# A piece of one V block sent as eight four-row transfers in a two-layer decode kernel

## The chip, the cores and the metric

The kernel runs on one core of a Trainium2 chip. The metric is the time of one execution on the device in microseconds (us), lower is better; a kernel is run several times and the median counts.

## The reference

One token passes through two layers. Each layer is attention over a cache, then a small dense block, both with a layer norm before and a residual after. Both layers use the same caches and weights.

```python
def _A_ref(x, k_cache, v_cache, wq, wo):        # 32 heads of 128, 4096 keys, x is 1 x 512
    q = (x @ wq).reshape(B, Sq, H, Dh).transpose(0, 2, 1, 3)
    scores = jnp.einsum("bhqd,bhkd->bhqk", q, k_cache) * (Dh ** -0.5)
    p = softmax(scores, axis=-1)
    o = jnp.einsum("bhqk,bhkd->bhqd", p, v_cache)
    return o.transpose(0, 2, 1, 3).reshape(B, Sq, H * Dh) @ wo
...
x = x + _A_ref(_layernorm(x), A_k_cache, A_v_cache, A_wq, A_wo)
x = x + _B_ref(_layernorm(x), B_w1, B_b1, B_w2, B_b2)    # gelu(x @ w1 + b1) @ w2 + b2, 1376 wide
x = x + _A_ref(...)
x = x + _B_ref(...)
```

## The kernel before

The 32 heads are worked on in 8 groups (`G`) of 4 heads (`J`). For a group the host lays K out as 128 rows of 64 KB (a row is one of a head's 128 dimensions) and V as 128 rows of 64 KB: row p holds keys p, p + 128, p + 256 and so on of the four heads. A block of 64 KB a row is eight chunks (`C`) of 2048 floats (`NC`); a chunk holds four pieces of 512 floats (`U`), and a piece is one run of 128 keys, 4 heads by 128 dimensions. One group reads K (8 MB), V (8 MB) and a row block of weights (2 MB: the group's wo and the next group's wq). Everything is float32.

All data goes into one large SBUF tile, `arena`. Its first three blocks are homes for K and V in turn (`k_home`, `v_home`); behind them lie spare chunks, `HELD` (first the start weights, at the layer's end the dense block's w1) and `PAIR` (wo and wq). `load` (L85) issues a transfer on SP's queue and keeps it in program order, so SP issues K, V and w of a group, then K, V and w of the next, each as soon as its home is free. The issue of w waits for the previous group's wo to be used up, which L311 does.

In the first six groups of layer 0 (the variable `pairs` is set) the V block isn't multiplied on TensorE. The softmax gives the weights `pt` with a key to a partition. ScalarE scales chunks 4 to 7 in 64 small instructions (`weighted_by_act`, L269), VectorE scales chunks 0 to 3 in four large ones (`weighted`, L274), and VectorE adds the chunks up: `add_pair` (L279) adds two chunks to two others and is called three times, 4096 columns each, and one addition of 2048 columns (L574) leaves the sum in the group's first chunk. Between these additions stands the next group's query (`queries`, L215 to L223). The sum over the partitions is taken late, in the middle of the next group's scores: `sum_over_keys` (L283, TensorE), `scaled_out` (L287 to L292) and `summed_wo` (L309 and L311, VectorE), and after that SP may issue the next w. The other groups multiply V on TensorE (L262).

GpSimd (POOL) prepares an identity matrix and a few constants at the start. Layer 1 goes through the groups in the opposite order and reads K and V again; it keeps what of the last group is still on the chip.

Of the kernel before, what the change touches and what calls it, by code (L numbers as in the profile page):

```python
# [13 lines left out]
AF = mybir.ActivationFunctionType  # L14
ALU = mybir.AluOpType
AX = mybir.AxisListType

P = 128
# [4 lines left out]
J = 4  # L23
C = 8
# [3 lines left out]
U = 512  # L28
KEPT = 6

NC = 4 * U
BLOCK = 8 * NC
# [3 lines left out]
HELD = SPARE + 2 * NC  # L36
PAIR = HELD + 4 * FJ * J
ARENA = PAIR + 2 * NC
SMALLS = 324
AHEAD = 64  # L40
X_AT, B1_AT, B2_AT = 0, 8, 8 + FB
K2_HOME = 12 * NC

# [11 lines left out]
WHOLE, HALVES = ((0, 8),), ((0, 4), (4, 8))  # L55
# [2 lines left out]


@with_exitstack  # L60
def decode_layers(ctx: ExitStack, tc: tile.TileContext, k, v, w, w1, w2, out):
    nc = tc.nc
    const = ctx.enter_context(tc.tile_pool(name="const", bufs=1))
    work = ctx.enter_context(tc.tile_pool(name="work", bufs=1))
# [2 lines left out]
    def ctile(name, *shape):  # L67
        return const.tile([P, *shape], F32, name=name)
# [14 lines left out]
    arena = const.tile([P, ARENA], F32, name="arena")  # L83

    def load(at, src):  # L85
        t = arena[:, at : at + src.shape[-1]]
        tc.keep_in_program_order(nc.sync.dma_start(t, src))  # L87
        return t

    def pin(ins):  # L90
        tc.keep_in_program_order(ins)

    def chunk(t, i=0):
        return t[:, NC * i : NC * (i + 1)].rearrange("p (j n) -> p j n", j=4)
# [12 lines left out]
    def free_now(layer, n):  # L107

        if layer == 0:
            at = HELD + 2 * NC  # L110
        elif n == 0:
            at = 6 * NC
            return arena[:, at : at + U], arena[:, 11 * NC : 11 * NC + 4 * 129]
        else:
            at = 9 * NC if n == 1 else 14 * NC
        return arena[:, at : at + U], arena[:, at + U : at + U + 4 * 129]
# [14 lines left out]
    ahead = load(HELD, w[row][:, : AHEAD + NC])  # L131
    wq_first = chunk(ahead[:, AHEAD:])

    ident = ctile("ident", P)
    make_identity(nc, ident)
    nc.vector.memset(negmean, -1.0 / D)
# [8 lines left out]
    pK = [psum.tile([P, U], F32, name=f"pK{j}") for j in range(KEPT - 1)]  # L145
# [7 lines left out]
    mx, mb = small("mx", 32), small("mb", 32)  # L153
    for t in (zq, mx, mb):
        nc.vector.memset(t, 0.0)

    def of_32(t, n, i=0):
        return t[:, : 32 * n].rearrange("p (c q) -> p c q", q=32)[:, :, i]
# [76 lines left out]
    def softmax(sc, nsc, p, hold):  # L235
        top = nc.vector.tensor_reduce(mx[:, 0:1], pS, axis=AX.X, op=ALU.max)  # L236
        if hold:
            pin(top)
        mt, m, bias = small("mt", 32), small("m"), small("lr", 32)
        nc.vector.transpose(mt, mx)  # L240
        nc.vector.tensor_reduce(m, mt[:, :C], axis=AX.X, op=ALU.max)
        nc.vector.tensor_scalar(mb[:, :C], m.to_broadcast([P, C]), nsc, None, op0=ALU.mult)
        nc.vector.transpose(bias, mb)  # L243
        nc.scalar.activation(p, pS, AF.Exp, bias=bias[:, 0:1], scale=sc, accum_out=mx[:, 0:1])  # L244
        for b in range(4):
            nc.tensor.transpose(pT[:, b].rearrange("p j r -> p (j r)"), p[:, P * b : P * (b + 1)], ident)  # L246
        pt = work.tile([P, J, C, 4], F32, name="pt")
        nc.vector.tensor_copy(pt, pT[:, :, :, :C].rearrange("p b j c -> p j c b"))
        lt, l, lr, rl = small("mt", 32), small("l"), small("lr", 32), small("rl")
        nc.vector.transpose(lt, mx)  # L250
        nc.vector.tensor_reduce(l, lt[:, :C], axis=AX.X, op=ALU.add)
        nc.vector.tensor_copy(lt, l.to_broadcast([P, 32]))
        nc.vector.transpose(lr, lt)
        nc.vector.reciprocal(rl, lr[:, 0:1])
        return pt, rl
# [4 lines left out]
    def values(i, pt, vt, c, of=C):  # L260
        for j in range(J):
            nc.tensor.matmul(pO[32 * j : 32 * j + 4, :], pt[:, j, c, :], by_head(vt)[:, j],  # L262
                             start=(i == 0), stop=(i == of - 1))

    def weighted_by_act(pt, t, c):
        for b in range(4):
            for j in range(J):
                own = by_head(t)[:, j, b]
                nc.scalar.activation(own, own, AF.Copy, scale=pt[:, j, c, b : b + 1])  # L269
# [3 lines left out]
        weight = pt[:, :, c, :].rearrange("p j b -> p b j")[:, :, :, None].to_broadcast([P, 4, J, DH])  # L273
        nc.vector.tensor_tensor(own, own, weight, op=ALU.mult)  # L274

    def add_pair(at, to, by):

        a, b = (arena[:, at + NC * c : at + NC * (c + 2)] for c in (to, by))
        pin(nc.vector.tensor_tensor(a, a, b, op=ALU.add))  # L279

    def sum_over_keys(t):
# [142 lines left out]
    here = {}  # L424

    def stream(what, g, pieces, base):

        for a, b in pieces:
            t = load(base + NC * a, part(k if what == "k" else v, g, a, b))
            for c in range(a, b):  # L430
                here[what, g, c] = chunk(t, c - a)
                yield c, here[what, g, c]
# [7 lines left out]
    for layer in range(2):  # L440
# [17 lines left out]
        r = rstd_of(ss, pN[:, 1:2], True)  # L458
# [5 lines left out]
        for n, g in enumerate(order):  # L464
            first, final = n == 0, n == G - 1
            pairs = None
            if layer == 0 and n < G - 2:
                pairs = PAIRS[0]
            if layer == 1 and 1 < n < G - 2:
                pairs = PAIRS[1][n % 2]  # L470

            k_home, v_home = ((2 * n + i) % 3 * BLOCK for i in (1, 2))
            if layer == 1:
                k_home, v_home = K2_HOME if n == 2 else 15 * NC, 6 * NC * (n % 2)
# [28 lines left out]
            p, ot = free_now(layer, n)  # L503
            if layer == 1 and first:
                z = queries(n + 1, xc_l, wq_next, pO)
                nc.scalar.copy(v_next(STAY + U * KEPT - U), pB)
            pt, rl = softmax(sc, nsc, p, held)
            if final:
                nc.scalar.activation(small("m"), rl, AF.Gelu_apprx_tanh)

            if layer == 1 and n == 0:
                for c in range(C):
                    values(c, pt, here["v", g, c], c)
            elif layer == 1 and n == 1:
                for c in range(C):
                    values(c, pt, here["v", g, c], c)

                for pieces, base in ((((0, 4),), K2_HOME), (((4, 6),), SPARE - 4 * NC)):
                    for _ in stream("k", order[2], pieces, base):
                        pass  # L520
            elif final:
                last_v = chunk(arena[:, v_home + BLOCK - NC : v_home + BLOCK])
                for _ in range(FILL - 1 if layer == 1 else 0):
                    idle(t, pS)
                for c, t in stream("v", g, LAST, v_home):
                    values(c, pt, t, c, C - 1)
                    if c == C - 2:
                        others = scaled_out(rl, ot)
                    for _ in range(LAST_IDLE.get(c, 0) * (1 + layer)):
                        idle(t, pS, 512 >> layer)  # L530
                for a, b in END_PARTS[layer]:
                    at = BLOCK - NC + U * a
                    load(v_home + at, v[g][:, at : BLOCK - NC + U * b])
                for c in range(C):
                    here["v", g, c] = chunk(arena[:, v_home + NC * c : v_home + NC * (c + 1)])
            else:
                for c, t in stream("v", g, WHOLE, v_home):
                    for i in range(KEPT - 1):
                        if layer == 0 and n == G - 2 and c == (STAY + U * i) // NC:
                            nc.scalar.copy(pK[i], t[:, STAY // U % J + i - J * (c - STAY // NC), :])  # L540
                    if pairs is None:
                        values(c, pt, t, c)
            if pairs:
                first_pair = pairs[0]
                for c in pairs[2:]:
                    for i in (0, 1):
                        weighted_by_act(pt, here["v", g, c + i], c + i)
                for c in pairs[:2]:
                    for i in (0, 1):
                        weighted(pt, here["v", g, c + i], c + i)  # L550
                add_pair(v_home, *pairs[:2])
# [3 lines left out]
            elif final:  # L555
                at = PAIR + NC * layer
# [9 lines left out]
            else:  # L566
                t = load(PAIR, of_w(wo_at(g) if layer == 0 else wq_at(g - 1), 2))
                wo_t, wq_next = (chunk(t, i) for i in ((0, 1) if layer == 0 else (1, 0)))
            if pairs:
                total, other = here["v", g, first_pair], here["v", g, first_pair + 1]  # L570
                z = queries(n + 1, xc_l, wq_next, pS, short=True,
                            between=lambda: add_pair(v_home, first_pair, pairs[2]))
                add_pair(v_home, first_pair, pairs[3])
                pin(nc.vector.tensor_tensor(total, total, other, op=ALU.add))  # L574

                def late_sum(rl=rl, ot=ot, wt=wo_t, total=total):
                    sum_over_keys(total)
                    summed_wo(scaled_out(rl, ot), wt, ot[:, :U])

                def late_out(ot=ot, n=n):  # L580
                    add_out(ot[:, :U], n)

                late = late_sum, late_out
                continue
# [24 lines left out]
        at = work.tile([P, P], F32, name="pt")  # L609
# [78 lines left out]
```

## Time and profile before

| what | value |
|---|---|
| median of 3 runs | 674.22 us (674.05 to 674.25) |
| profiled execution | 673.33 us |
| its span, first to last instruction | 671.6 us |
| busy in the span: TensorE, VectorE, ScalarE, GpSimd | 299.7, 407.1, 215.4, 5.2 us |
| moved by DMA | 285.29 MB, mean 425 GB/s |

Busy time is that of instructions on an engine within the profiled execution's span. The profiled execution takes some 2 us more than its span, for what lies before the first and after the last instruction.

### The profile page before, as it was taken

How to read it: one execution, taken by the hardware profiler on the slowest of the kernel's cores; microseconds unless marked ns; L12 is line 12 of the kernel's file. 1: busy time of each engine (PE TensorE's matmuls, PEld its weight loads, DVE VectorE, ACT ScalarE, POOL GpSimd, SP SyncE). 2: the span in 40 equal slices, each digit the busy share in tenths (PEclk: the TensorE clock that was granted, in tenths of full speed). 3: DMA queues.
4: the chain of work that ended last, by engine and by line, in shares of the span. 5: the costliest groups of instructions: out<-in, count | busy, mean ns of one | idle time of the engine just before them, and what ended most of it. 6: DMA issues, size and time to landing. Idle time of an engine off the chain costs nothing.

```text
span 671.6 us, 6013 instructions
## 1 busy us (share of the span) xinstructions
PE 299.7 (45%) x2236; PEld 79.7 (12%) x2236; DVE 407.1 (61%) x510; ACT 215.4 (32%) x697; POOL 5.2 (1%) x26
## 2 busy tenths in 40 slices
PE   1511703415116053165768986704316025065597
PEld 1000100101001010011114311101001001011124
DVE  3059679498696886971322313288597694973513
ACT  0047074190560823802011200083290650910010
POOL 1000000000000000000000000000000000000000
PEclk9965755757558557578689998655757559557799
DMA  9999999999999999999999999999999999999997
GB/s 377 437 437 438 435 437 437 403 461 437 437 437 397 444 426 434 433 429 426 425 415 399 422 422 438 437 433 433 431 433 437 437 430 402 462 426 414 431 414 286
DMA packets 11556, 285.29 MB, mean 425 GB/s; under 512 B 1284, under 2 KB 1288, under 8 KB 3720
## 3 DMA queue, kind: packets, MB, share of 16 engines
q1 hardware_dynamic: 11528, 284.92, 99.1%
q8 instruction: 17, 0.28, 0.2%
q14 instruction: 11, 0.09, 0.0%
HBM read 284.92 MB, written 0.00 MB: 424 GB/s over the span
## 4 chain that ended last, share of the span: by engine, by line
DMA 64%; PE 17%; DVE 15%; issue 1%; another core or an unknown queue 1%; SPq 1%; ACT 0%; DVEq 0%; ACTq 0%
DMA arena<-in_v 37%; DMA arena<-in_k 24%; PE pS L232 8%; DVE arena L274 7%; PE pO L262 5%; DMA arena<-in_w 4%; DVE arena L279 3%; DVE arena L311 2%; PE pO L283 1%; DVE arena L287 1%; DVE arena L215 1%; SPq L87 1%; PE pB L323 1%; DVE arena L309 0%
## 5 line engine op out<-in xcount | busy, mean ns | idle before, releaser
L269 ACT ACTIVATE arena<-arena,pt 128x128 f32<-128x128 f32 x640 | 188.0, 387 | 50.8 <-DMA arena<-in_v 48.1
L232 PE MATMUL pS<-arena,smalls 128*8 128x512 f32 x1024 | 147.0, 727 | 78.4 <-DMA arena<-in_k 74.3
L279 DVE TENSOR_TENSOR arena<-arena 128x4096 f32<-128x4096 f32 x30 | 132.6, 4420 | 0.3
L274 DVE TENSOR_TENSOR arena<-arena,pt 128x2048 f32<-128x2048 f32 x40 | 89.0, 2287 | 36.8 <-DMA arena<-in_v 35.7
L217 PE MATMUL pS<-arena,smalls 128*128 128x512 f32 x20 | 20.7, 1140 | 202.5 <-DVE arena L215 202.5
L244 ACT ACTIVATE arena<-pS,smalls 128x512 f32<-128x512 f32 x16 | 12.4, 777 | 289.4 <-DVE smalls L243 289.4
L287 DVE STREAM_TRANSPOSE arena<-pO 128x512 f32<-128x512 f32 x16 | 11.5, 717 | 97.4 <-PE pO L262 61.9
L262 PE MATMUL pO<-arena,pt 128*4 128x512 f32 x368 | 48.9, 666 | 11.8 <-DMA arena<-in_v 11.0
L232 PEld LDWEIGHTS pS<-arena,smalls 128*8 128x8 f32 x1024 | 29.8, 102 | 198.6 <-issue 177.3
L236 DVE TENSOR_REDUCE smalls<-pS 128x1 f32<-128x512 f32 x16 | 11.0, 687 | 64.1 <-PE pS L232 64.1
L215 DVE SCALAR_TENSOR_TENSOR arena<-arena,smalls 128x512 f32<-128x512 f32 x45 | 33.8, 752 | 1.6
L311 DVE SCALAR_TENSOR_TENSOR arena<-arena,smalls 128x512 f32<-128x512 f32 x39 | 29.3, 752 | 1.4
L217 PEld LDWEIGHTS pS<-arena,smalls 128*128 128x128 f32 x20 | 5.0, 311 | 206.2 <-DVE arena L215 206.2
L315 PE MATMUL pB<-arena,smalls 128*1 128x512 f32 x26 | 14.7, 648 | 29.0 <-DVE arena L311 29.0
L246 PE MATMUL pO<-ident,arena 128*128 128x128 f32 x64 | 13.4, 344 | 28.1 <-ACT arena L244 27.8
L574 DVE TENSOR_TENSOR arena<-arena 128x2048 f32<-128x2048 f32 x10 | 22.9, 2292 | 0.3
L382 ACT ACTIVATE smalls<-smalls 128x4 f32<-128x4 f32 (+1 forms) x6 | 1.2, 205 | 44.0 <-DVE smalls L375 25.6
L262 PEld LDWEIGHTS pO<-arena,pt 128*4 128x4 f32 x368 | 9.8, 93 | 44.8 <-issue 42.4
L250 DVE STREAM_TRANSPOSE smalls<-smalls 128x32 f32<-128x32 f32 x16 | 3.4, 212 | 17.5 <-ACT arena L244 17.5
L246 PEld LDWEIGHTS pO<-ident,arena 128*128 128x128 f32 x64 | 8.4, 167 | 42.1 <-ACT arena L244 36.7
L244 ACT ACT_TABLE_LOAD x1 | 1.3, 1283 | 36.9 <-DVE smalls L243 36.9
L438 PE MATMUL pS<-arena,ident 128*8 128x256 f32 (+1 forms) x34 | 11.9, 454 | 0.5 <-DVE pt L367 0.5
(115 smaller groups left out, 183.6 us busy)
## 6 DMA issues: line engine op xcount, KB each, us to landing
arena<-in_w SPq DMA_DIRECT2D x13, 2048.0 KB, 12.5
arena<-in_k SPq DMA_DIRECT2D x6, 4096.0 KB, 21.3
arena<-in_v SPq DMA_DIRECT2D x2, 4096.0 KB, 25.1
arena<-in_w SPq DMA_DIRECT2D x6, 1024.0 KB, 30.9
arena<-in_v SPq DMA_DIRECT2D x2, 2048.0 KB, 37.0
arena<-in_k SPq DMA_DIRECT2D x2, 2048.0 KB, 13.4
arena<-in_w SPq DMA_DIRECT2D x7, 512.0 KB, 9.3
arena<-in_v SPq DMA_DIRECT2D x3, 1024.0 KB, 46.3
```

The costliest lines, as they stand in the source:

```text
L215: pin(nc.vector.scalar_tensor_tensor(t, wt[:, c, :], xc[:, c : c + 1], t, op0=ALU.mult, op1=ALU.add))
L217: pin(nc.tensor.matmul(at, one.to_broadcast([P, P]), t, start=True, stop=True))
L232: pin(nc.tensor.matmul(pS[32 * j : 32 * j + C, :], z[:, j, C - 1 - c : 2 * C - 1 - c], kt[:, j, :], start=(c == 0), stop=(c == C - 1)))
L246: nc.tensor.transpose(pT[:, b].rearrange("p j r -> p (j r)"), p[:, P * b : P * (b + 1)], ident)
L262: nc.tensor.matmul(pO[32 * j : 32 * j + 4, :], pt[:, j, c, :], by_head(vt)[:, j], start=(i == 0), stop=(i == of - 1))
L269: nc.scalar.activation(own, own, AF.Copy, scale=pt[:, j, c, b : b + 1])
L274: nc.vector.tensor_tensor(own, own, weight, op=ALU.mult)
L279: pin(nc.vector.tensor_tensor(a, a, b, op=ALU.add))
L287: nc.vector.transpose(ot[:, :512], pO)
L311: pin(nc.vector.scalar_tensor_tensor(t, wt[:, d, :], on[:, d : d + 1], t, op0=ALU.mult, op1=ALU.add))
L315: pin(nc.tensor.matmul(pB[0:1, :], one, t, start=n == 0, stop=n == G - 2))
L574: pin(nc.vector.tensor_tensor(total, total, other, op=ALU.add))
```

## The change

The last piece (128 keys of each of the four heads, 512 floats a row) of the V block of group 4, the fifth, no longer comes with the block in layer 0. The host lays the same 256 KB out a second time, as an array `m` of 48 rows of 8 KB, in which rows 0 to 15 and 32 to 47 hold data: a row there holds the four heads' values of four keys. Eight transfers bring them into `low`, an area of 48 partitions by 2048 columns that POOL clears at the start. Each takes 4 rows, four partitions apart: rows 0, 4, 8, 12; then 1, 5, 9, 13; and so on, and the same from row 32. Two of them are issued on SP's queue behind V in each of the groups 0 to 3. In group 4 the V block is loaded without its last 512 columns; the weights of the moved keys are turned onto the 48 partitions by four TensorE transposes and a copy (`low_weights`), ScalarE scales `low` in 16 small instructions and leaves out the 4 of the piece that is gone (`weighted_low`), the third `add_pair` is 512 columns shorter, and VectorE adds `low` to the first 48 partitions of the group's sum. A few scratch places move. Layer 1 reads the V block as before.

```diff
+LOW = 48
+MOVED_OF = 4
+MOVED_AT = HELD + NC + AHEAD
+MOVED_ROWS = [slice(32 * h + q, 32 * h + q + 13, 4) for h in range(2) for q in range(4)]
...
         if layer == 0:
-            at = HELD + 2 * NC
+            at = MOVED_AT + NC
...
+    low = arena[:LOW, MOVED_AT : MOVED_AT + NC]
+    nc.gpsimd.memset(low, 0.0)
     ident = ctile("ident", P)
     make_identity(nc, ident)
...
+    low_pt = arena[:, PAIR - 4 * J : PAIR]
...
-    def weighted_by_act(pt, t, c):
-        for b in range(4):
+    def low_weights(p):
+        at = pK[0][:LOW]
+        for i in range(4):
+            first = 3 * P + 64 * (i // 2) + 16 * (i % 2)
+            nc.tensor.transpose(at[:, P * i : P * (i + 1)], p[:, first : first + LOW], ident)
+        t = low_pt[:LOW].rearrange("p (i j) -> p i j", i=4)
+        nc.vector.tensor_copy(t, at.rearrange("p (i j r) -> p i j r", i=4, j=J)[:, :, :, C - 1])
+        return t
+
+    def weighted_low(t):
+        own = low.rearrange("p (i j d) -> p i j d", i=4, j=J)
+        for i in range(4):
+            for j in range(J):
+                nc.scalar.activation(own[:, i, j], own[:, i, j], AF.Copy, scale=t[:, i, j : j + 1])
+
+    def weighted_by_act(pt, t, c, of=4):
+        for b in range(of):
...
-    def add_pair(at, to, by):
-
-        a, b = (arena[:, at + NC * c : at + NC * (c + 2)] for c in (to, by))
+    def add_pair(at, to, by, short=0):
+
+        a, b = (arena[:, at + NC * c : at + NC * (c + 2) - short] for c in (to, by))
         pin(nc.vector.tensor_tensor(a, a, b, op=ALU.add))
...
             pt, rl = softmax(sc, nsc, p, held)
+            dealt = layer == 0 and n == MOVED_OF
+            if dealt:
+                pt_low = low_weights(p)
...
-                for c, t in stream("v", g, WHOLE, v_home):
+                if dealt:
+                    load(v_home, v[g][:, : BLOCK - U])
+                    pieces = [(c, chunk(arena[:, v_home + NC * c : v_home + NC * (c + 1)])) for c in range(C)]
+                    here.update({("v", g, c): t for c, t in pieces})
+                else:
+                    pieces = stream("v", g, WHOLE, v_home)
+                for c, t in pieces:
...
+            if layer == 0 and n < MOVED_OF:
+                for rows in MOVED_ROWS[2 * n : 2 * n + 2]:
+                    pin(nc.sync.dma_start(low[rows], m[rows]))
             if pairs:
                 first_pair = pairs[0]
                 for c in pairs[2:]:
                     for i in (0, 1):
-                        weighted_by_act(pt, here["v", g, c + i], c + i)
+                        weighted_by_act(pt, here["v", g, c + i], c + i, 3 if dealt and c + i == C - 1 else 4)
+                if dealt:
+                    weighted_low(pt_low)
...
-                add_pair(v_home, first_pair, pairs[3])
+                add_pair(v_home, first_pair, pairs[3], U if dealt else 0)
                 pin(nc.vector.tensor_tensor(total, total, other, op=ALU.add))
+                if dealt:
+                    of_low = arena[:LOW, v_home + NC * first_pair : v_home + NC * (first_pair + 1)]
+                    pin(nc.vector.tensor_tensor(of_low, of_low, low, op=ALU.add))
...
+    moved = arrays["v"][MOVED_OF, :, BLOCK - U : BLOCK].reshape(2, 2, 2, 16, U)
+    arrays["m"] = np.zeros((LOW, 4, U), np.float32)
+    for i in range(4):
+        for h in range(2):
+            arrays["m"][32 * h : 32 * h + 16, i] = moved[i // 2, h, i % 2]
+    arrays["m"] = arrays["m"].reshape(LOW, NC)
```

## Rows read from the trace of the kernel before

**Rows 1.** The page: span, packets, bytes by DMA queue.
```profile
span 671.6 us, 6013 instructions
...
DMA packets 11556, 285.29 MB, mean 425 GB/s; under 512 B 1284, under 2 KB 1288, under 8 KB 3720
...
q1 hardware_dynamic: 11528, 284.92, 99.1%
```

**Rows 2.** The page: chain that ended last, by engine.
```profile
DMA 64%; PE 17%; DVE 15%; issue 1%; another core or an unknown queue 1%; SPq 1%; ACT 0%; DVEq 0%; ACTq 0%
```

**Rows 3.** Busy time and DMA, windows; DMA share and GB/s stand last.
```profile
88.00:300.00 212.00, 67.55 (x394) 15.65 (x394) 169.91 (x149) 97.48 (x328) 0.00 (x0) 0.61 1.00 433
```

**Rows 4.** Timeline of SP's queue, groups five and six: start, us, issue.
```profile
212.58 0.33 SPq L87 DMA_DIRECT2D arena<-in_w  x1
...
256.79 0.33 SPq L87 DMA_DIRECT2D arena<-in_w  x1
```

**Rows 5.** DMA, window 43.40:44.00.
```profile
DMA packets 32, 0.26 MB, mean 437 GB/s; under 512 B 16, under 2 KB 16, under 8 KB 16
```

**Rows 6.** DMA, window 305.1:305.7.
```profile
DMA packets 20, 0.16 MB, mean 273 GB/s; under 512 B 10, under 2 KB 10, under 8 KB 10
```

**Rows 7.** DMA, window 305.7:306.9.
```profile
DMA packets 20, 0.33 MB, mean 273 GB/s; under 512 B 0, under 2 KB 0, under 8 KB 0
```

**Rows 8.** DMA, window 306.9:307.5.
```profile
DMA packets 22, 0.26 MB, mean 437 GB/s; under 512 B 6, under 2 KB 6, under 8 KB 6
```

**Rows 9.** DMA queues, window 5:361.9.
```profile
q8 instruction: 7, 0.11, 0.1%
q14 instruction: 5, 0.04, 0.0%
```

**Rows 10.** The chain, end of layer 0: start us, us, what.
```profile
360.18 7.25 DMA arena<-in_w
...
367.57 1.00 PE pO L414 x24
```

**Rows 11.** DMA, window 668.9:671.6.
```profile
DMA packets 8, 0.00 MB, mean 1 GB/s; under 512 B 4, under 2 KB 8, under 8 KB 8
...
out<-arena SPq DMA_DIRECT2D x1, 2.0 KB
```

**Rows 12.** DMA, window 354:359.
```profile
DMA packets 290, 2.11 MB, mean 423 GB/s; under 512 B 32, under 2 KB 32, under 8 KB 32
```

**Rows 13.** DMA, window 261.3:262.0.
```profile
DMA packets 19, 0.21 MB, mean 304 GB/s; under 512 B 9, under 2 KB 9, under 8 KB 9
```

**Rows 14.** DVE timeline, fifth group.
```profile
220.34 8.90 DVE L274 TENSOR_TENSOR arena<-arena,pt 128x2048 f32<-128x2048 f32 x4 [3.89 <-DMA arena<-in_v]
...
242.04 4.42 DVE L279 TENSOR_TENSOR arena<-arena 128x4096 f32<-128x4096 f32 x1
...
246.49 2.29 DVE L574 TENSOR_TENSOR arena<-arena 128x2048 f32<-128x2048 f32 x1
...
252.64 0.72 DVE L287 STREAM_TRANSPOSE arena<-pO 128x512 f32<-128x512 f32 x1 [3.87 <-PE pO L283]
```

**Rows 15.** ACT timeline, fifth group.
```profile
220.34 18.80 ACT L269 ACTIVATE arena<-arena,pt 128x128 f32<-128x128 f32 x64 [5.28 <-DMA arena<-in_v]
...
258.40 0.78 ACT L244 ACTIVATE arena<-pS,smalls 128x512 f32<-128x512 f32 x1 [19.27 <-DVE smalls L243]
```

**Rows 16.** PE timeline, fifth and sixth group.
```profile
215.11 0.94 PE L246 MATMUL pO<-ident,arena 128*128 128x128 f32 x4 [1.52 <-ACT arena L244]
...
251.53 1.04 PE L283 MATMUL pO<-arena,smalls 128*4 128x512 f32 x8
```

**Rows 17.** POOL timeline, start.
```profile
5.72 0.19 POOL L422 COPY smalls<-arena 128x11 f32<-128x11 f32 x1 [4.37 <-DMA arena<-in_w]
```

**Rows 18.** The chain, start of the kernel.
```profile
0.72 4.95 DMA arena<-in_w
```

More of the change, by code (lines that the diff above doesn't have):

```diff
@@ L60, in decode_layers @@
 @with_exitstack
-def decode_layers(ctx: ExitStack, tc: tile.TileContext, k, v, w, w1, w2, out):
+def decode_layers(ctx: ExitStack, tc: tile.TileContext, k, v, w, w1, w2, m, out):
     nc = tc.nc
```

## The prediction

> **What bounds the kernel now.** I read the page first, for the resource that is full, then the windows and SP's queue, for whether it ever runs dry, and last narrow windows of the DMA view, for how evenly its sixteen engines finish.
>
> The transfers take 99.1% of sixteen engines' span [rows 1], and DMA is 64% of the chain that ended last [rows 2]. Over 212 us of layer 0 the DMA share is 1.00 at 433 GB/s [rows 3]. Fifteen transfers end in that stretch, so a transfer behind another costs nearly nothing: all that is missing to the 437 GB/s of a stretch without an end is 212 x 4/437 = 1.9 us, 0.13 us for each end at the most. The queue doesn't run dry: SP issues the next round at 212.58 and 256.79 [rows 4], while earlier transfers still run.
>
> So layer 0 takes as long as its slowest DMA engine. An engine closes its share of a transfer with a small packet: 1284 packets are under 512 B [rows 1], 80 x 16 + 4. Their count in a window is the number of engines that ended a transfer there. The first V block is ended by all sixteen within 0.6 us [rows 5]. The V block of the seventh group is ended by ten in 0.6 us [rows 6], by none in the next 1.2 us [rows 7], and by six in the 0.6 us after that [rows 8]. Some engines have fallen 1.2 to 2.4 us behind, and a consumer waits for all sixteen. The reader sees one cause in the queues: up to 361.9 us seven packets of q8 and five of q14 carried instructions [rows 9]; each delays the one engine that it comes on. The rate here is 437/16 = 27.3 GB/s for an engine, and a late one has no gap in which to catch up. At the end of layer 0 the chain stands on such a transfer: the load issued at 360.18 lands 7.25 us later, and the matmuls start 0.14 us after that [rows 10]. What the slowest engine gains or loses before that, the kernel gains or loses.
>
> **The bytes, step by step.** Removed: 512 floats, 2 KB, of each of 128 rows of the fifth V block, 256 KB, 16 KB for each engine. At 27.3 GB/s that is 0.60 us less for each of the sixteen. Added: the same 256 KB as eight transfers of 4 rows of 8 KB. The trace before has one transfer of 4 rows, the store of the result: four packets of 512 B and four small ones [rows 11], so one row to an engine and twelve engines without work. If all eight take the same four engines, each of these gets 64 KB: 2.40 us at 437 GB/s. In a stretch of transfers with 8 KB rows the rate is 423 GB/s [rows 12], which makes it 2.48 us. Net, four engines get 1.80 to 1.88 us more and twelve get 0.60 us less.
>
> No view names the engine of a packet, so which four is not to be read. The Trainium skill says it ("DMA: Bandwidth & Descriptors", the section on why a DMA increments its semaphore by 16): a transfer issued from SP runs on the largest number of engines up to 16 that divides its row counts, and on the lowest-numbered of them. The store agrees on the number four; no run here shows the lowest-numbered.
>
> The price depends on whether one of the four is late already. If one of them is the latest, the end moves by the whole 1.80 to 1.88. If it is the first of the six late ones, it goes from 306.9 to 308.7 or more against a latest of at most 307.5: 1.2. I take 1.7, near the upper end, since with several engines in the group the latest of them counts, and between 306 us and the end of the layer more engines become late (seven q8 packets, rows 9, each 16 KB: 0.11 MB/7). Bounds: 1.2 and 1.9.
>
> **The work that goes with it.** All lies beside other work:
> - SP issues eight more DMAs, 0.33 us each [rows 4], 2.6 us over four rounds of some 44 us, in which it mostly waits. They go in ahead of w of the same group and K of the next. What is queued behind them is needed tens of us later.
> - In the fifth group DVE's last addition ends at 246.49 + 2.29 = 248.78 [rows 14]. It gets one more addition over 2048 columns: 48 lanes, but time goes by columns, so 2.29 us by the same row, and it loses 512 of the 4096 columns of one that takes 4.42, so 0.55. Ends at 250.5. PE wants the sum at 251.53 [rows 16]: 1.0 us of cover is left. Without it the delay goes on to the sixth group's w issue at 256.79, and there is a second cover: the first engines end V of the sixth group only between 261.3 and 262.0 [rows 13], 4.5 us after the issue.
> - ACT scales 16 small pieces more and 4 less. 18.80 us/64 is 0.29 each [rows 15], 3.5 us more: it ends at 242.7, before DVE takes up the new addition after 248.2; then it is idle to 258.40. DVE's addition at 242.04 needs only the first 60: 238.0.
> - PE makes four more transposes, 0.94 us [rows 16], and DVE one small copy, bounded by 0 and the 2.29 us of a far larger addition. DVE is idle 3.89 us there, waiting for V [rows 14].
> - POOL clears the 48 x 2048 area first. No row shows one so large; the bounds are 0 and 2.29 us as for DVE's pass over as many columns. POOL is idle for 4.37 us before 5.72 [rows 17], and so it takes nothing.
>
> Sum: the profiled execution's 673.33 + 1.7 = 675.0, and as the median of the runs is 674.22, 0.9 us above it, 675.9 for the median. That is slower by 0.25%; a measurement of this kernel can tell about 0.2%, 1.35 us, from no change.
>
> **Rivals.**
> *All four engines are among the early ones.* Then they go from 305.1-305.7 to 306.9-307.6 and the late ones from 306.9-307.5 to 306.3-306.9: the latest changes by between -0.6 and +0.1. I take -0.2: 674.0, not slower. For it: q8's seven packets seem to come on an engine each, which would make the late ones neighbours, and the four might lie outside their run. Against it: drawn at random, four of sixteen miss six late ones in 210 of 1820 cases, 12%, and the code packets of the 50 us that follow make more engines late. It decides from the point where no engine of the four is late by more than some 0.1 us. I give 0.36.
> *The transfers wait for one another.* All write one area whose rows interleave. If a wait is put between them, SP stands at the second of each pair until the first has landed, behind a whole V block, and issues nothing for the next round: four times the queue runs dry. A dry start is bounded by the first load: 4.95 us [rows 18] for 1.08 MB, of which 2.47 is its bytes at 437 GB/s, so 2.5 us each, 10 us: 684.2. Against it: the rows are distinct. 0.05. The Trainium skill has a rule that speaks against the change in the same way ("DMA: Bandwidth & Descriptors", "Rules for kernel authors"): transfers under 64 KB are mostly overhead, with about 2 us of fixed cost. Were that paid eight times on the queue, the estimate by that page is 16 us; the trace doesn't agree for transfers behind others, 0.13 us an end [rows 3].
> *The rows spread over sixteen engines after all*, by splitting or by going to other engines each time: bytes as before, 674.2. The store's four packets speak against it. 0.04.
>
> **How the numbers follow.** One of the four late: 0.52, its own range 675.4 to 676.2 (and 0.04 of it under the 0.2% mark). All four early 0.36, spread 0.04, waiting 0.05; 0.03 is for a gain that I can't name, since 0.6 us is all that the bytes can give. Slower: 0.48 + 0.05 = 0.53. Same: 0.36 + 0.04 + 0.04 = 0.44. Faster 0.03. The range takes in both large cases, from 674.22 - 0.6 = 673.6 to 674.22 + 1.9 + 0.3 for the spread of a run = 676.4, and leaves out the waiting.
>
> **What would show it.** Packets under 512 B: 1284 + 32 = 1316, with 32 more of 8 KB, and SP with two more issues behind V in each of the first four groups and no long wait between them. In the sixth and seventh groups' V, a few engines that end 1.8 us or so after the latest of before against twelve that end 0.6 us sooner; if the four were early, all sixteen end closer together. The load at the end of layer 0 lands later by the whole difference, and layer 1 takes what it took. DVE's last addition of the fifth group ends near 250.5 and ACT's run is 22.3 us long. I am wrong if the four are early, if the queue runs dry in the first four rounds, or if the fifth group's tail delays SP's issue past 261.

## The result, and the profile after

The changed kernel takes 676.31 us (median of 6 runs, 675.25 to 677.97) against 674.22 us (6 runs, 673.75 to 674.54): ratio 1.0033, 95% interval 1.002 to 1.0047, so 2.2 us slower, with 1.3 to 3.2 as bounds. The profiled execution took 675.25 us, 1.92 more than that of before, and its span 673.5 us, 1.9 more. Differences below are (ratio - 1) x 674.2.

The page of the changed kernel answers to [rows 1]. It has 64 packets more, 32 of them small, and moves the same bytes:
```profile
span 673.5 us, 6056 instructions
...
DMA packets 11620, 285.29 MB, mean 424 GB/s; under 512 B 1316, under 2 KB 1320, under 8 KB 3752
```

The windows of the changed kernel, same stretch as [rows 3] (DMA share and GB/s last), show the queue as full as before. Wherever the time went, it wasn't to a queue that ran dry:
```profile
88.00:300.00 212.00, 68.25 (x398) 15.70 (x398) 170.89 (x150) 100.98 (x340) 0.00 (x0) 0.63 1.01 433
```

SP's timeline of the changed kernel (start, us, instruction) shows the pairs of new transfers and the w behind them, which answers to [rows 4]:
```profile
12.04 1.40 SPq L577 DMA_DIRECT2D arena<-in_m  x2
...
78.50 1.23 SPq L577 DMA_DIRECT2D arena<-in_m  x2
81.69 0.33 SPq L91 DMA_DIRECT2D arena<-in_w  x1
...
214.97 0.33 SPq L91 DMA_DIRECT2D arena<-in_w  x1
```
Where the delay arises is read from the chain: at the start of a group's scores TensorE waits for that group's K. These are the lines of the third to the seventh group before:
```profile
113.78 5.73 PE pS L232 x40
...
157.40 6.11 PE pS L232 x40
...
201.01 6.49 PE pS L232 x40
...
245.07 6.64 PE pS L232 x40
...
288.70 7.01 PE pS L232 x40
```
The same lines in the changed kernel:
```profile
114.27 6.81 PE pS L240 x40
...
158.91 6.68 PE pS L240 x40
...
203.16 6.74 PE pS L240 x40
...
246.86 7.07 PE pS L240 x40
...
290.49 5.75 PE pS L240 x40
```
The differences are +0.49, +1.51, +2.15, +1.79 and +1.79 us, with two, three and four pairs sent ahead of the first three of these K. The delay is thus on the transfers and grows with the pairs sent: 2.15 us stand after the eighth transfer, before a single instruction of the new arithmetic has run (PE's transposes start at 218.00). Then comes the V block that lost 16 KB for each engine, which VectorE takes up at 221.93 where before it was 220.34 [rows 14], +1.59. SP's issues of w are a poorer mark, since the 40 matmuls above, which take 5.73 to 7.07 us, lie ahead of them: +2.39 at 214.97, +2.23 at 259.02 and +0.52 at the next, 301.31.

Four narrow windows of the DMA view of the changed kernel, from 305.1 us on, follow the V block of the seventh group, as [rows 6], [rows 7] and [rows 8] do; the last is split further and shows its part from 308.7:
```profile
DMA packets 9, 0.16 MB, mean 273 GB/s; under 512 B 2, under 2 KB 2, under 8 KB 2
...
DMA packets 26, 0.44 MB, mean 369 GB/s; under 512 B 5, under 2 KB 5, under 8 KB 5
...
DMA packets 15, 0.21 MB, mean 355 GB/s; under 512 B 2, under 2 KB 2, under 8 KB 2
...
DMA packets 18, 0.26 MB, mean 437 GB/s; under 512 B 2, under 2 KB 2, under 8 KB 2
```
The small packets count engines that end: 2 in 305.1-305.7, 5 in 305.7-306.9, 2 in 306.9-307.5, and the last 2 only in 308.7-309.3 (4 end before 305.1 and one at 307.5-308.1). Before, the last six ended in 306.9-307.5. So the block's last engine is some 1.8 us later, while others have become earlier. Two engines share that last window, so a second one of the four is close behind the latest.

The chain at the end of layer 0 answers to [rows 10]: the transfer lands at 369.21, where before it landed at 367.43.
```profile
362.14 7.07 DMA arena<-in_w
...
369.21 0.14 issue
369.35 0.62 PE pO L437 x16
...
370.49 0.33 DVE pt L672
```
The last of these lines is VectorE's first work behind that load. In the chain of before it stands 1.84 us earlier, and I use it as the mark of layer 0's end:
```profile
368.65 0.33 DVE pt L632
```
From there to the end of the span it is 303.0 us in both: layer 1 is unchanged.

### The profile page after: what moved, and what is told of

It reads as the page before. It is cut to its first block, busy times and chain, and to the rows that moved or that the text cites. A ratio compares the mean times of both kernels' runs of the same rounds, so it can differ in the third digit from the quotient of the medians.

```text
span 673.5 us, 6056 instructions
## 1 busy us (share of the span) xinstructions
PE 297.8 (44%) x2240; PEld 80.4 (12%) x2240; DVE 408.5 (61%) x512; ACT 218.9 (32%) x709; POOL 7.0 (1%) x27
## 4 chain that ended last, share of the span: by engine, by line
DMA 64%; PE 17%; DVE 15%; issue 1%; another core or an unknown queue 1%; SPq 1%; ACT 0%; DVEq 0%; ACTq 0%
DMA arena<-in_v 37%; DMA arena<-in_k 23%; PE pS L240 8%; DVE arena L297 7%; PE pO L270 5%; DMA arena<-in_w 3%; DVE arena L302 3%; DVE arena L334 2%; PE pO L306 1%; DVE arena L310 1%; DVE arena L223 1%; SPq L91 1%; PE pB L346 1%; DVE arena L332 0%
## 5 line engine op out<-in xcount | busy, mean ns | idle before, releaser
L302 DVE TENSOR_TENSOR arena<-arena 128x4096 f32<-128x4096 f32 (+1 forms) x30 | 132.0, 4401 | 0.3
```

## The experiments

All times are medians; each ratio is to the kernel before on the same chip.

| run | us | ratio (95% interval) | difference, us |
|---|---|---|---|
| compute_alone | 674.17 | 1.0005 (0.9996 to 1.0014) | +0.3 |
| dma_alone | 676.58 | 1.0038 (1.0026 to 1.0051) | +2.6 |
| probe_1 | 674.55 | 1.0013 (1.0004 to 1.0022) | +0.9 |
| probe_2 | 676.60 | 1.0038 (1.0024 to 1.0052) | +2.6 |
| probe_4 | 676.51 | 1.0037 (1.0025 to 1.005) | +2.5 |
| eight_rows | 676.71 | 1.0045 (1.0033 to 1.0057) | +3.0 |
| eight_apart | 675.00 | 1.0013 (1.0004 to 1.0021) | +0.9 |
| probe_4_high | 680.11 | 1.0086 (1.007 to 1.0103) | +5.8 |
| sent_twice | 690.70 | 1.0252 (1.0239 to 1.0265) | +17.0 |
| act_more | 692.53 | 1.0276 (1.0254 to 1.0297) | +18.6 |
| act_more_4 | 692.67 | 1.0279 (1.0257 to 1.03) | +18.8 |
| act_late | 675.93 | 1.0034 (1.0022 to 1.0045) | +2.3 |
| act_late_4 | 678.65 | 1.0071 (1.0057 to 1.0086) | +4.8 |
| act_late_2 | 678.63 | 1.0075 (1.0058 to 1.0091) | +5.1 |
| by_pool | 749.35 | 1.1119 (1.1104 to 1.1134) | +75.4 |

**Which half of the change costs?** compute_alone keeps the new arithmetic and takes the new transfers out:
```diff
-                    load(v_home, v[g][:, : BLOCK - U])
+                    load(v_home, v[g][:, :BLOCK])
...
-            if layer == 0 and n < MOVED_OF:
-                for rows in MOVED_ROWS[2 * n : 2 * n + 2]:
-                    pin(nc.sync.dma_start(low[rows], m[rows]))
```


> The fifth V block is loaded whole again and the eight small transfers are not issued; all the new instructions on TensorE, ScalarE, VectorE and GpSimd stay. It leaves the last 128 keys of that group's four heads out of layer 0. Theory (the bytes on four late DMA engines are the cause): 674.2, within 0.3 of before. Rival (the longer tail of the fifth group on ScalarE and VectorE, or the code that it adds): 675.5 to 676.5, as the whole change.

dma_alone keeps the transfers and takes the arithmetic out (`low_weights`, `weighted_low`, the short addition and the addition of `low`).


> The eight small transfers and the shorter V load stay, the new instructions on the other engines go; the last 128 keys of the fifth group are then weighted from stale data, and the moved ones are read by nobody. Theory: 676.3, the whole loss. Rival: 674.2.

compute_alone is within what can be told from no change, and dma_alone costs as much as the whole change. The mark of layer 0's end, in the traces of the two, says the same more sharply: +0.04 and +1.96 us against before.
```profile
368.69 0.33 DVE pt L669
...
370.61 0.33 DVE pt L667
```
The loss is in the transfers.

**Which engines?** The probes are the arithmetic and V block of before, with eight unread transfers of one, two or four 8 KB rows added in the same places. The cut shows probe_1; probe_2 has + 5 in place of + 1, and probe_4 the + 13 of the change:
```diff
-MOVED_ROWS = [slice(32 * h + q, 32 * h + q + 13, 4) for h in range(2) for q in range(4)]
+MOVED_ROWS = [slice(32 * h + q, 32 * h + q + 1, 4) for h in range(2) for q in range(4)]
...
-            dealt = layer == 0 and n == MOVED_OF
+            dealt = False
```


> The kernel before, its V load whole and none of the new arithmetic, plus eight transfers of 1 row of 8 KB that nobody reads, at the places of the change's transfers. They can only go to one engine, which gets 64 KB, 8 x 0.32 = 2.6 us. Theory (one-row transfers go to the first engine, which reads no code in layer 0 and is some 2.2 us early at the end of the layer): 674.4, +0.2 to +0.6. Rival (eight more transfers cost by themselves): as probe_4.

> As probe_1 with 2 rows to a transfer, 64 KB more on each of two engines. Theory (the second engine also reads VectorE's code and is 0.15 us from the latest): +2.4, 676.5. Rival (the first two engines are both early and only the fourth is late): as probe_1.

> As probe_1 with the change's own eight transfers of 4 rows, 64 KB more on each of four engines and nothing taken away. Theory (the fourth engine reads ScalarE's code and is the latest): +2.6, 676.7. Rival (bytes on late engines don't count in full): under +1.5.

One row at a time costs 0.9 us, two rows 2.6, and four no more than two. The mark of layer 0's end stands 0.49, 2.65 and 2.66 us later than before in the three traces:
```profile
369.14 0.33 DVE pt L672
...
371.30 0.33 DVE pt L672
...
371.31 0.33 DVE pt L672
```
The three pages have 16, 32 and 64 packets more than before, so each row comes as one 8 KB packet with a small one that closes it, on one engine. The bytes for one engine are then the same 64 KB in all three, and so is the number of transfers. So the engine that the one-row transfers use has room, some 1.7 us by the times and 2.2 by the marks, and one that the second row brings in has none. SP issues the second to fourth pair 40 to 45 us earlier in probe_1 than in the other two (33.74 against 78.97 and 79.01 for the second), but in all three behind the same V, so I take it that the place in the queue is the same; no run shows that by itself. That each larger set holds the smaller agrees with the Trainium skill ("DMA: Bandwidth & Descriptors", the section on why a DMA increments its semaphore by 16), by which a transfer takes the lowest-numbered engines.

**Half the bytes on twice the engines.** eight_rows sends the moved keys as four transfers of 8 rows:
```diff
-MOVED_ROWS = [slice(32 * h + q, 32 * h + q + 13, 4) for h in range(2) for q in range(4)]
+MOVED_ROWS = [slice(32 * h + q, 32 * h + q + 15, 2) for h in range(2) for q in range(2)]
...
-                for rows in MOVED_ROWS[2 * n : 2 * n + 2]:
+                for rows in MOVED_ROWS[n : n + 1]:
```


> The same 256 KB in four transfers of 8 rows, one behind V in each of the groups 0 to 3. If 8 rows go to eight engines, each of these gets 32 KB more and 16 KB less, 0.6 us net, where the four got 1.8 to 1.9. Theory: +0.6, 674.8. Rival (the number of transfers costs, not the bytes): half the loss, +1.0. Rival (compute): 676.3.

This missed: 3.0 us where 0.6 was expected. The rows stand two partitions apart there. eight_apart also has four transfers of 8 rows, but puts the 256 KB on partitions 0 to 31, rows four partitions apart:
```diff
-LOW = 48
+LOW = 32
...
-MOVED_ROWS = [slice(32 * h + q, 32 * h + q + 13, 4) for h in range(2) for q in range(4)]
+MOVED_ROWS = [slice(q, q + 29, 4) for q in range(4)]
...
-                for rows in MOVED_ROWS[2 * n : 2 * n + 2]:
+                for rows in MOVED_ROWS[n : n + 1]:
```


> The change with its 256 KB laid on partitions 0 to 31 and sent as four transfers of 8 rows, four partitions apart, so that eight engines write to eight groups of four partitions, where in eight_rows they wrote to four. Output as the reference's. Theory (each of eight engines gets 1.2 us more and 0.6 less): +0.6 to +0.8, 674.9. Rival (a transfer of 8 rows costs by itself): +2.7, as eight_rows.

With the same bytes and the same number of rows it costs 0.9, by these differences 2.1 us less than eight_rows, near the 2.5/2 - 0.6 = 0.65 of half the bytes. The windows of eight_rows, same stretch as before, show the rate lower at a full queue; eight_apart has 434 GB/s there:
```profile
88.00:300.00 212.00, 66.58 (x390) 15.78 (x394) 169.72 (x148) 100.98 (x340) 0.00 (x0) 0.62 1.00 430
```
So besides bytes on an engine there is a price for where they are written. probe_4_high is probe_4 with the rows written to partitions 64 to 79 and 96 to 111:
```diff
+    high = arena[64 : 64 + LOW, MOVED_AT : MOVED_AT + NC]
...
-                    pin(nc.sync.dma_start(low[rows], m[rows]))
+                    pin(nc.sync.dma_start(high[rows], m[rows]))
```


> probe_4 with the rows written to partitions 64 to 79 and 96 to 111. The engines are the same if they are chosen by the number of rows, and the partitions are those that other engines write. Theory: +2.6 as probe_4, or more by what two writers to the same partitions cost each other (20 long packets, some 4 us over all engines in eight_rows). Rival (partitions choose the engines): other engines, and another time.

5.8 us against 2.5 for the same rows on low partitions. Its rate over the same stretch is the lowest of the three:
```profile
88.00:300.00 212.00, 64.09 (x346) 14.29 (x350) 166.43 (x142) 97.47 (x328) 0.00 (x0) 0.62 1.01 427
```
The kept traces hold each packet's own time, which no view lists. Of the 1024 packets of 16 KB in layer 0, half take up to 0.614 us. None took over 0.8 us before, 5 did in the changed kernel, 2 in probe_4, 1 in eight_apart, but 52 in eight_rows, all of them near 44, 88, 132 and 177 us, where a V block ends and the small transfers run, and 137 in probe_4_high, most of them near the same times. So where the small rows are written slows the packets of other transfers beside them. That it is the same partitions that engines hold one another up at is argued from these times, since no view and no packet names them.

**What would waiting cost?** sent_twice issues each pair of transfers a second time, to the same place:
```diff
-                for rows in MOVED_ROWS[2 * n : 2 * n + 2]:
+                for rows in 2 * MOVED_ROWS[2 * n : 2 * n + 2]:
```


> Each of the eight transfers is issued a second time with the same data. Four engines get another 64 KB, 2.4 to 2.5 us. Theory (one of the four is the slowest engine, so each byte on it counts in full): 678.8. Rival (the four are late for another reason and have slack): under 677.

This missed by 12 us: the second issue waits for the landing of the first. SP's waits in that run (us in total, times, longest) and its timeline:
```profile
SPq L577 <- DMA arena<-in_m: 59.8, 4, 31.0
```
```profile
12.07 33.62 SPq L577 DMA_DIRECT2D arena<-in_m  x4
45.73 0.44 SPq L91 DMA_DIRECT2D arena<-in_w  x1
```
SP stands for 33 us, and w goes out 32 us later than the 13.47 of the changed kernel. That is the second rival of the prediction, made real: four waits, and 17.0 us with the change and the doubled bytes in it. The changed kernel has no such wait.

**Why is that engine late?** Code reads were the suspect [rows 9]. To the kernel before, its V block and arithmetic, act_more adds 64 one-column instructions of ScalarE in each of the first six groups, act_more_4 the eight four-row transfers as well:
```diff
+                if layer == 0:
+                    for _ in range(64):
+                        spare = low_pt[:, :1]
+                        nc.scalar.activation(spare, spare, AF.Copy, scale=1.0)
```


> The kernel before with 64 ScalarE instructions of one column more in each of the first six groups, 384 in all, after the group's own; no small transfers. ScalarE's code is read 8 KB for about 128 instructions, so some three more reads of its code fall into layer 0. Theory (ScalarE's code always comes on the same DMA engine, and a read and the packet after it take 0.7 us there): +1.5 to +2.1, 676. Rival (code reads are spread or cost nothing): 674.2.

> act_more and probe_4 together. Theory (the engine that reads ScalarE's code is among the four that take the small transfers): the two add up, +4.1 to +4.7, 678.6. Rival (it is another engine): the larger of the two, +2.6, 676.8.

Both missed and tell nothing of code reads. Windows of act_more (ScalarE's busy time is the fourth, DMA share the last but one):
```profile
45.00:90.00 45.00, 10.37 (x46) 2.49 (x46) 28.83 (x20) 41.50 (x177) 0.00 (x0) 0.55 0.94 406
90.00:135.00 45.00, 7.83 (x40) 2.08 (x40) 27.42 (x30) 38.72 (x161) 0.00 (x0) 0.61 0.88 373
135.00:180.00 45.00, 19.08 (x112) 4.31 (x116) 41.78 (x36) 19.67 (x66) 0.00 (x0) 0.64 0.82 349
```
The instructions, which depended on nothing, ran in the first groups ahead of the scalings; ScalarE became the bound and the queue ran dry. In act_late the added instructions, 56 a group, read the group's weights and are held in place behind the scalings; act_late_4 and act_late_2 add the eight transfers of four and of two rows:
```diff
+                if layer == 0:
+                    for _ in range(56):
+                        pin(nc.scalar.activation(low_pt[:, :1], pt[:, 0, 0, :1], AF.Copy, scale=1.0))
```


> The kernel before, with 56 one-column ScalarE instructions more in each of the first six groups, held in their place behind that group's 64 scalings, where ScalarE is otherwise idle for some 19 us; they read the group's weights and write one unread column. 64 instructions of about 0.2 us a group did cost ScalarE some 13 us in the run before this one; 56 take some 11 us of the 19, so nothing on the engines should be late. They are 336 instructions more to be read in: two to three 8 KB code reads on q14, each about 0.7 us (0.32 us for the read, 0.38 us of a longer block packet behind it). Theory (all of ScalarE's code reads come on one DMA engine, the fourth, which is among the two latest when layer 0 ends): plus 1.4 to 2.1 us, 675.6 to 676.3. Rival (the reads go from engine to engine, or come on an engine with room): plus 0 to 0.7, 674.2 to 674.9.

> The run with 56 more ScalarE instructions a group and, behind V of the first four groups, the eight unread four-row transfers of 8 KB rows of the probe, which alone cost 2.6 us. Theory (ScalarE's code reads come on one of the four engines that take the rows): the two add up on one engine, 2.6 + 1.4 to 2.1 = 4.0 to 4.7, 678.2 to 678.9. Rival (they come on another engine): the larger alone counts, 2.6, 676.8.

> The same with two-row transfers, which alone cost 2.4 to 2.6 us on the first two engines. Theory (ScalarE's code reads come on the fourth engine, the first two are slowed by VectorE's, on the second): the larger counts, 2.4 to 2.6, 676.6 to 676.9, some 1.4 to 2 us under the four-row run of the same call. Rival (ScalarE's reads come on one of the first two): as much as the four-row run, 678.2 to 678.9.

ScalarE's timeline in act_late, fifth group: the new run ends at 253.2 and ScalarE then is idle for 5.67 us, so the new instructions hold nothing up on ScalarE.
```profile
221.38 18.80 ACT L293 ACTIVATE arena<-arena,pt 128x128 f32<-128x128 f32 x64 [6.01 <-DMA arena<-in_v]
240.09 13.08 ACT L585 ACTIVATE arena<-pt 128x1 f32<-128x1 f32 x56
258.84 0.78 ACT L253 ACTIVATE arena<-pS,smalls 128x512 f32<-128x512 f32 x1 [5.67 <-DVE smalls L252]
```
In the DMA queues of act_late from 5 to 364 us there are three code reads more than [rows 9] has, 8 KB each:
```profile
q14 instruction: 8, 0.07, 0.0%
```
And in its DMA windows 306.9:307.5 and 309.3:309.9 five engines and then a single one end V of the seventh group, the last some 2 us behind all others, where before none was left after 307.5:
```profile
DMA packets 21, 0.31 MB, mean 519 GB/s; under 512 B 5, under 2 KB 5, under 8 KB 5
...
DMA packets 17, 0.26 MB, mean 437 GB/s; under 512 B 1, under 2 KB 1, under 8 KB 1
```
The other ten end by 306.3, and before ten ended by 305.7 [rows 6]. The counts fit one of the six late engines having become later, and no other. Three code reads of 8 KB cost the kernel 2.3 us, 0.76 each (1.99 at the mark of layer 0's end), and this points to one engine for all three. With the four-row transfers the prices add up (4.8 is 2.3 + 2.5), and with the two-row ones too (5.1); the marks are +4.72 and +4.65. The last was a miss: I had put ScalarE's reads on the fourth engine. They come on one of the first two, and as the first isn't among the late ones (probe_1), the second. That is an inference from four times and the windows; no view gives the engine's name. By it, of the change's four engines this one sets the end.

**Can the reads be taken away?** by_pool lets GpSimd scale chunks 4 to 7 in four large instructions, which takes 640 instructions out of ScalarE's stream:
```diff
-    def weighted(pt, t, c):
+    def weighted(pt, t, c, by=nc.vector):
...
-                        weighted_by_act(pt, here["v", g, c + i], c + i)
+                        weighted(pt, here["v", g, c + i], c + i, nc.gpsimd)
```


> The kernel before, in which GpSimd scales chunks 4 to 7 in four instructions of 2048 columns where ScalarE did it in 64 (full output). It takes some 640 instructions out of ScalarE's stream: 384 in layer 0, which by the run with 336 more are about three 8 KB code reads of 0.73 us each on one DMA engine. Theory (that engine is the latest at the end of layer 0, and the next latest is close to 1 us behind it in the trace before): minus 0.7 to 1.4 us in layer 0, 672.4 to 673.1, and no more, since then the engine of another code read is the latest. Rival: a GpSimd pass over 2048 columns, which no run shows, takes over 5 us or slows VectorE's additions beside it, so that the sum of a group comes after SP's queue needs it: slower, and SP stands at w for it.

The rival came. GpSimd takes 22.67 us a group, near ScalarE's 18.80, but VectorE beside it takes twice as long. VectorE's timeline of by_pool, second group:
```profile
95.59 19.22 DVE L274 TENSOR_TENSOR arena<-arena,pt 128x2048 f32<-128x2048 f32 x4
114.84 7.74 DVE L279 TENSOR_TENSOR arena<-arena 128x4096 f32<-128x4096 f32 x1
...
125.26 4.42 DVE L279 TENSOR_TENSOR arena<-arena 128x4096 f32<-128x4096 f32 x1
```
The four scalings took 8.90 before [rows 14]; the addition that runs beside GpSimd takes 7.74, the one after it 4.42. VectorE is full and the DMA share falls to 0.85 in 88-300 us. No version here beats the kernel before.

## Why the prediction was right or wrong

**What bounds the kernel: right.** The queue stayed full and the slowest engine set the end of layer 0, at the mark 1.84 us later; layer 1 took the same 303.0 us.

**One of the four engines is the latest: right**, the forecast's own case, though at a chance of 0.52 it was little better than a coin. The prediction left open which and why; the probes and act_late put it on the second engine, loaded by ScalarE's code reads, which is argued and not read from a view. The third and fourth add nothing to the time (probe_4 against probe_2).

**The size of the term: the step that failed.** The prediction took 1.7 for the price, under its own net of 1.80 to 1.88, to allow for a late engine that is not quite the latest, and ended its range at 1.9 + 0.3 = 2.2, 676.4. Measured is 2.2, which by the ratio is 674.22 x 1.0033 = 676.44, just above that edge. The engine is the latest, so there was nothing to take off: at the mark of layer 0's end the change stands 1.84 us later, and dma_alone 1.96. The full net was the right value, though its two parts were both too small. The added rows alone stand 2.65 and 2.66 later (probe_2, probe_4) where 2.40 to 2.48 was forecast, and against them the change, with its 16 KB less for each engine, gives back 0.7 to 0.8 and not 0.60. At the fifth group's K the rows had cost less than forecast (2.15 in the changed kernel, 2.18 and 2.25 in the two probes), and in the probes the excess appears after that, with no new transfer left; what makes it stays open.

The other 0.3, from 1.92 in the profiled executions to 2.2, lies in part between them and the medians, which differ by 2.09 (the changed kernel's profiled execution is the lowest of six runs that spread over 2.7 us), and in part in how the ratio is formed. What was wrong in the range is that 1.9 was held to be a bound on what the runs show. It was a bound in one execution, and 0.3 around it was less than the runs have. With an interval of 1.3 to 3.2 the time alone can't tell 1.9 from 2.2.

**The side work costs nothing: right** (compute_alone, +0.3, interval across zero). In the changed kernel's VectorE timeline the last two additions run
```profile
247.53 2.29 DVE L611 TENSOR_TENSOR arena<-arena 128x2048 f32<-128x2048 f32 x1
249.85 2.28 DVE L614 TENSOR_TENSOR arena<-arena 48x2048 f32<-48x2048 f32 x1
254.86 0.72 DVE L310 STREAM_TRANSPOSE arena<-pO 128x512 f32<-128x512 f32 x1 [2.73 <-PE pO L306]
```
and end at 252.13, later than the forecast 250.5 by what V came later, 1.59 us; 48 lanes take as long as 128, as forecast (2.28 and 2.29). PE takes the sum up at 253.75. ScalarE ran the 16 small pieces first, 4.78 + 17.62 = 22.4 us with 22.3 forecast, and ends at 241.6. SP's price of an issue was too low, 1.23 us for two instead of 0.66, without effect. SP does stand for up to 43.7 us ahead of the new transfers, but it stood as long at the w behind them before.

**The rivals.** All four early: fell. Spread over sixteen: fell by the probes, since a row more or less changes the time. Waiting for one another: did not happen; sent_twice, which has four such waits and the bytes twice, cost 17.0 where the rival had 10. The Trainium skill's rule against small transfers ("DMA: Bandwidth & Descriptors", "Rules for kernel authors") has them mostly overhead under 64 KB; at the 2 us each of the prediction's estimate eight of them would be 16 us (the page fits that figure to transfers issued from GpSimd; these are issued from SP). probe_1's eight cost 0.9 in all, bytes included, so for transfers queued behind others the runs don't agree.

## What to carry to other kernels

When the DMA queue is always full, count bytes by engine, not in total: a transfer of few rows loads few engines, and moving 256 KB from sixteen of them to four cost about what the four got more. Ask which engine is already behind (the small closing packets in narrow windows show how many are), and add or remove rows of a probe transfer to learn whether the new bytes meet it. If they do, the full net counts, and the range has to allow for the spread of runs around one profiled execution. Compare traces at a mark behind the last transfer that the change touches: there compute_alone differs from before by 0.04 us, while whole runs spread over 2 us and more.

## What the runs showed of the hardware that was not expected

- ScalarE's code is read by the DMA engines that carry the data. With 336 more small instructions in layer 0 there are three 8 KB reads more and one engine is some 2 us later, which cost 2.3 us: small instructions have a price on the DMA side even where ScalarE is idle.
- Where rows are written counts beside their bytes: 8 rows two partitions apart cost 3.0 us and four apart 0.9; four rows on partitions 64 and up 5.8, on 0 and up 2.5. In the dear cases 52 and 137 packets of other transfers took over 0.8 us instead of 0.614, in the cheap ones 1 and 2.
- GpSimd passes beside VectorE passes double the latter: 19.22 instead of 8.90 us for four scalings.
